# Attention and ResMLP over eight batches: W1's chunks taken forwards and backwards in turn, and the third batch's k, q and v loaded and flipped one pass earlier

## The chip, the cores and the metric

The kernel runs on one core of a Trainium2 chip. The time is the device time of one execution in microseconds (us), and the median of several executions is compared. The profile is that of one execution: its span runs from the first to the last instruction. The engines are PE (TensorE's matmuls; PEld is its weight loads), DVE (VectorE), ACT (ScalarE), POOL (GpSimd) and SP (SyncE); the last two mostly issue DMAs here.

## The reference

For each of eight batches, grouped-query attention is computed and its output goes through a ResMLP block. The shapes are 16 query heads, 4 key heads, 384 positions and 64 elements per head, so that the attention output is 384 x 1024; W1 is 1024 x 4096 and W2 is 4096 x 1024. Everything comes in and goes out as float32.

```python
attn = softmax(q @ k.T / sqrt(D)) @ v            # each key head serves four query heads
x = attn.transpose(0, 2, 1, 3).reshape(B, S, H * D)
a1 = alpha1 * x + beta1
u = x + lam * einsum('ts,bsd->btd', w_tok, a1)
a2 = alpha2 * u + beta2
out = u + lam * (maximum(a2 @ w_ch1, 0.0) @ w_ch2)
```

## The kernel before

After a lead in which the first batch's attention and token mixing are done (`side(0)`), there are eight passes, one for each batch. Pass b is `main(b)`: the **first product** h = relu(a2 @ W1), L417 to L452, and the **second product** ch = h @ W2 with the output, L453 to L469. While it runs, the attention and token mixing of batch b + 1 (`side(b + 1)`) are set between its matmuls.

The first product takes 32 column blocks `nt` of 128 columns. Each is eight matmuls (L424) of a W1 block with a2T (384 columns; 385 in the first pass), then a bias and a relu on ACT or DVE into hT, which holds all 32 blocks. Two blocks are a **chunk** of W1 (512 KB in bfloat16), so there are 16 chunks. W1 is not kept: a ring of six tiles (`RING`) is refilled on POOL's queue by DMAs that read float32 and write bfloat16 (`load_w1`, L149). When chunk c is used up, its slot takes the chunk six further on. At the end of a pass that is the first six chunks of the next one (L438 and L439; L445 to L447 in the first pass). W2 is loaded once: three of its 16 parts in the lead, thirteen after chunk 10 of the first pass (L440 to L444), all of them at L154. The second product (L461) has six groups of 32 matmuls with 512 columns, in the order of `nt`; its output is scaled and added by DVE (L466, L467) and written by SP (L468).

The order of instructions is written by hand and holds for each engine's queue. `main` is a generator that yields after each few matmuls; the yields of the first product count the units of one list, those of the second product the units of another. `side(b + 1)` gives the two lists, from unit to work. For most batches the list for the first product is empty. For batch 1 it has the key and query transposes on TensorE with `k_transpose` (L208) and `q_transpose` (L218) in units 8 to 40, for batch 2 the query transposes in units 24, 32, 40 and 48 (L368). A `q_transpose` is six matmuls and a copy by DVE.

From batch 3 on (and for batch 2's k) there are no transposes on TensorE. q, k and v are loaded on POOL's queue (`load_q` L131, `load_k` L106, `load_v` L125; `load_next` does all three) and k and q are turned by transposing DMAs on SP's queue (`flip_k` L134, `flip_q` L138). These are added to the lists in L605 to L610: load in unit 2 of the second product of pass b for batch b + 2, `flip_k` in unit 34, `flip_q` in units 36, 37, 42 and 43. Batch 2 is apart: k is loaded at the end of the first pass (L448), q after chunks 1 to 4 and v after chunk 10 of the second pass (L449 to L452), and k is flipped in unit 1 of the second pass. a2 goes to a2T by transposing DMAs on SP too (L312), in the second product, one for each of eight slices.

The tiles `q_raw` and `k2` have one buffer each, v has two (`vt`). All the waits between engines, for loads and for buffers, are set by the framework from which instruction reads or writes what.

Of the kernel before, what the change touches and what calls it, by code (L numbers as in the profile page):

```python
# [12 lines left out]
def kernel(  # L13
# [21 lines left out]
    nc = tc.nc  # L35
    f32 = mybir.dt.float32
# [12 lines left out]
    P = 128  # L49
# [22 lines left out]
    ident = const.tile([P, P], bf, tag="ident", name="ident")  # L72
    vt = [const.tile([P, NST, Hkv, D1], bf, tag=f"v{i}", name=f"v{i}") for i in range(2)]
    w2 = const.tile([P, NNT, DM], bf, tag="w2", name="w2")
    hT = const.tile([P, NNT, S], bf, tag="hT", name="hT")
    hTf = hT.rearrange("p n s -> p (n s)")
    vecs = const.tile([P, 4, DM], f32, tag="vecs", name="vecs")
# [45 lines left out]
    def load_v(b, sts=range(NST)):  # L123
        for st in sts:
            nc.gpsimd.dma_start(out=vt[b % 2][:, st, :, :D], in_=by_st(v[b])[:, st])  # L125

    def load_q(b, hs=range(0, Hq, G)):
        if b not in qrs:
            qrs[b] = sb.tile([P, Hq, NST, D], bf, tag="q_raw", name="q_raw", bufs=1)
        for h in hs:  # L130
            nc.gpsimd.dma_start(out=qrs[b][:, h:h + G], in_=q[b, h:h + G].rearrange("h (p st) d -> p h st d", st=NST))  # L131

    def flip_k(b):
# [6 lines left out]

    w1src = moe_w_ch1.rearrange("(dt di) nf -> di dt nf", di=P)
    w2src = moe_w_ch2.rearrange("(nt ni) d -> ni nt d", ni=P)
    w1_tiles = {}

    def load_w1(n):
        if n < B * NCH:
            t = sb.tile([P, NDT, CW * P], bf, tag="w1", name="w1", bufs=RING)
            c = n % NCH
            nc.gpsimd.dma_start(out=t, in_=w1src[:, :, c * CW * P:(c + 1) * CW * P])  # L149
            w1_tiles[n] = t  # L150

    def load_w2(dw, i, n):
        r, cs = slice(i * NNT // n, (i + 1) * NNT // n), slice(dw * 512, (dw + 1) * 512)
        nc.gpsimd.dma_start(out=w2[:, r, cs], in_=w2src[:, r, cs])  # L154

    def bank(shape, tag, name, dtype=f32):
        if tag == "three":
            return threes[0].tile(shape, dtype, tag="sc", name=name, bufs=3)
        if tag == "mm":
            return mms.tile(shape, dtype, tag="mm", name=name, bufs=2)  # L160
        return psum.tile(shape, dtype, tag=tag, name=name, bufs=2 if tag == "sc" else 1)

    def three():
        return bank([P, 2, 4, P], "three", "sc")

    def tp_ps(shape, tag="tp"):
        return bank(shape, tag, "tp", bf)
# [9 lines left out]
    def h_part(nts, dts):  # L177
        for nt in nts:
            if nt % 2 == 0 and nt not in early:
                t = bank([P, 2, 512], "sc", "h")  # L180
                early[nt], early[nt + 1] = t[:, 0], t[:, 1]
            for dt in dts:
                nc.tensor.matmul(out=early[nt][:, :S + 1], lhsT=w1_tiles[nt // CW][:, dt, nt % CW * P:(nt % CW + 1) * P],  # L183
                                 rhs=a2Ts[0][:, dt, :S + 1], start=(dt == 0), stop=(dt == NDT - 1))


# [2 lines left out]
    def side(b):  # L189
# [175 lines left out]
        if not first:  # L365


            turns = {24 + 8 * i: [(q_transpose, 2 * i, 2, "three")] for i in range(4)} if b == 2 else {}  # L368
            if b == 1:
                turns = {4: [(to_all, 3, 0, 0), (to_all, 3, 1, 1), (load_row_set, 1, 1, 0), (load_row_set, 2, 0, 1)],  # L370
                         8: [(k_transpose, 0)], 12: [(to_all, 1, 0, 2), (to_all, 1, 1, 0), (load_row_set, 2, 1, 0)],
                         16: [(scale_beta,)], 20: [(to_all, 2, 0, 1), (to_all, 2, 1, 0)],
                         24: [(q_transpose, 0, 2, "av")], 28: [(k_transpose, 2)]}
                for i in range(3):
                    turns[32 + 4 * i] = [(q_transpose, 2 + 2 * i, 2, "av")]
            return turns, {
                0: [(scores3, 0)], 4: [(av, 0)], 6: [(scores3, 1)], 8: [(tok_flip, 0)], 11: [(av, 1)],
                13: [(scores3, 2, True)], 15: [(av, 2)], 16: [(tok_flip, 1)], 18: [(tok_flip, 2)], 19: [(av, 3)],
                21: [(scores3, 3)], 23: [(tok_flip, 3)], 25: [(av, 4)], 27: [(scores3, 4)], 29: [(tok_flip, 4)],
                31: [(av, 5)], 33: [(scores3, 5, True)], 35: [(av, 6), (tok_flip, 5)], 37: [(av, 7)],  # L380
                39: [(tok_flip, 6)], 41: [(tok_flip, 7)]}
# [31 lines left out]
    def main(b):  # L413
        a2T = a2Ts[b % 2]
        x = xs.pop(b)
        n = S + 1 if b == 0 else S
        for c in range(NCH):  # L417
            w1 = w1_tiles.pop(b * NCH + c)
            for j in range(CW):
                nt = c * CW + j  # L420
                begun = b == 0 and nt in early
                ps = early[nt] if begun else bank([P, 512], "mm", "h")
                for dt in range(0 if begun else NDT):
                    nc.tensor.matmul(out=ps[:, :n], lhsT=w1[:, dt, j * P:(j + 1) * P],  # L424
                                     rhs=a2T[:, dt, :n], start=(dt == 0), stop=(dt == NDT - 1))
                    if dt == 3:
                        yield 0
                c1 = bias1[:, nt:nt + 1]
                if b == 0:
                    evac("DVE" if nt % 2 else "ACT")(out=c1, in_=ps[:, S:n])  # L430
                if nt % 2 == 0:
                    nc.scalar.activation(out=hT[:, nt, :], in_=ps[:, :S], func=RELU, bias=c1)  # L432
                else:
                    nc.vector.tensor_scalar(out=hT[:, nt, :], in0=ps[:, :S], scalar1=c1,  # L434
                                            scalar2=0.0, op0=ADD, op1=mybir.AluOpType.max)
                yield 0

            if b or c + RING < NCH:  # L438
                load_w1(b * NCH + c + RING)  # L439
            if b == 0 and c == NCH - RING:  # L440
                for i in range(3, 8):
                    load_w2(0, i, 8)
                for i in range(8):
                    load_w2(1, i, 8)  # L444
            if b == 0 and c == NCH - 1:  # L445
                for i in range(RING):
                    load_w1(NCH + i)  # L447
                load_k(2)  # L448
            if b == 1 and c in range(1, 5):  # L449
                load_q(2, [G * (c - 1)])  # L450
            if b == 1 and c == NCH - RING:
                load_v(2)  # L452
        for dw in range(NDW):  # L453
            cs = slice(dw * 512, (dw + 1) * 512)
            for ms in range(NST):
                ps = bank([P, 512], "mm", "ch")
                o = sb.tile([P, 512], f32, tag="tmp", name="o", bufs=4)
                last = (b, dw, ms) == (B - 1, NDW - 1, NST - 1)
                for lo, hi in ((0, 256), (256, 384), (384, 512)) if last else ((0, 512),):
                    for nt in range(NNT):  # L460
                        nc.tensor.matmul(out=ps[:, lo:hi], lhsT=hT[:, nt, ms * P:(ms + 1) * P],  # L461
                                         rhs=w2[:, nt, dw * 512 + lo:dw * 512 + hi], start=(nt == 0), stop=(nt == NNT - 1))
                        if nt % 4 == 3 and nt < NNT - 1:
                            yield 1
                    c = slice(dw * 512 + lo, dw * 512 + hi)
                    nc.vector.tensor_tensor(out=o[:, lo:hi], in0=ps[:, lo:hi], in1=lam_t[:, c], op=MUL)  # L466
                    nc.vector.tensor_tensor(out=o[:, lo:hi], in0=o[:, lo:hi], in1=x[:, ms, c], op=ADD)  # L467
                    nc.sync.dma_start(out=out[b].rearrange("(p st) d -> p st d", st=NST)[:, ms, c], in_=o[:, lo:hi])  # L468
                yield 1  # L469
# [3 lines left out]
    with tc.manual_schedule(engines=order):  # L473
# [128 lines left out]
        place_k(1, 1)  # L602
        for b in range(B):
            us = side(b + 1) if b + 1 < B else ({}, {})
            moves = [(0, 1, flip_k, 2)] if b == 1 else []  # L605
            if 0 < b < B - 2:
                moves += [(1, 2, load_next, b + 2), (1, 34, flip_k, b + 2), (1, 36, flip_q, b + 2, 0, 2),
                          (1, 37, flip_q, b + 2, 2, 2), (1, 42, flip_q, b + 2, 4, 2), (1, 43, flip_q, b + 2, 6, 2)]
            for i, u, *m in moves:
                us[i].setdefault(u, []).append(m)  # L610
            done = [0, 0]
            for second in main(b):
                if b == second - done[1] - 1 == 0:
                    lead_banks.close()
                    threes.append(ST(tc.psum_pool(name="threes", bufs=3)))
                for f, *a in us[second].get(done[second], []):
                    f(*a)
                done[second] += 1
# [28 lines left out]
```

## Time and profile before

| what | value |
|---|---|
| median of four runs | 802.69 us (801.8 to 802.83) |
| the profiled execution | 802.28 us |
| its span | 800.5 us |
| granted TensorE clock | 1.0 |
| HBM read / written | 172.92 MB / 12.58 MB |
| loads of W1 (L149) and W2 (L154) | 128 and 16, 512 KB each |
| starts of the first products, from the chain | 37.8, 131.5, 229.5, 326.2, 422.8, 519.5, 616.1, 712.8 us |

The profile has several views. The page gives each engine's busy time and share, and the span in 40 slices (tenths of a slice that the engine was busy, tenths of the clock that was granted, DMA load). The chain of waits follows the work that ended last back from the last instruction; in order of time it gives pieces by start, length, engine and line. Views by stretch give busy time between two moments, views by engine list instructions, and the view of waits says who waited for whom. For a DMA the trace has its issue and the time from issue to landing.

### The profile page before, as it was taken

How to read it: one execution, taken by the hardware profiler on the slowest of the kernel's cores; microseconds unless marked ns; L12 is line 12 of the kernel's file. 1: busy time of each engine (PE TensorE's matmuls, PEld its weight loads, DVE VectorE, ACT ScalarE, POOL GpSimd, SP SyncE). 2: the span in 40 equal slices, each digit the busy share in tenths (PEclk: the TensorE clock that was granted, in tenths of full speed). 3: DMA queues.
4: the chain of work that ended last, by engine and by line, in shares of the span. 5: the costliest groups of instructions: out<-in, count | busy, mean ns of one | idle time of the engine just before them, and what ended most of it. 6: DMA issues, size and time to landing. Idle time of an engine off the chain costs nothing.

```text
span 800.5 us, 14229 instructions
## 1 busy us (share of the span) xinstructions
PE 793.7 (99%) x6131; PEld 452.7 (57%) x6131; DVE 347.3 (43%) x676; ACT 223.1 (28%) x302; POOL 181.4 (23%) x232
## 2 busy tenths in 40 slices
PE   8999999999999999999999999999999999999997
PEld 5765555655556555565555655566555655556545
DVE  7663555226542266323662235622465225552122
ACT  7623340232412332123221234122421223312100
POOL 9434311451013400235002340033300330003000
PEclk9999999999999999999999999999999999999999
DMA  9999999999279963999439992599914994139411
GB/s 191 197 199 203 213 205 147 184 195 178 58 133 185 197 98 69 151 189 196 84 82 143 197 199 49 101 156 198 175 47 114 177 197 80 47 67 182 57 40 40
DMA packets 234875, 112.42 MB, mean 140 GB/s; under 512 B 87348, under 2 KB 228644, under 8 KB 234812
## 3 DMA queue, kind: packets, MB, share of 16 engines
q0 software_dynamic: 177088, 85.83, 81.6%
q1 hardware_dynamic: 57180, 25.29, 12.8%
q8 instruction: 48, 0.79, 0.4%
q10 hardware_dynamic: 544, 0.39, 0.2%
q14 instruction: 15, 0.12, 0.0%
HBM read 172.92 MB, written 12.58 MB: 232 GB/s over the span
## 4 chain that ended last, share of the span: by engine, by line
PE 98%; DVE 2%; issue 0%; ACT 0%
PE ch L461 42%; PE h L424 41%; PE sc L232 4%; PE sc L267 4%; PE sc L290 4%; PE h L183 1%; PE tp L218 1%; PE tok L290 0%; PE av L267 0%; PE warm L478 0%; PE ut L307 0%; DVE x L273 0%; DVE vecs L348 0%; PE tok L294 0%; DVE hT L545 0%
## 5 line engine op out<-in xcount | busy, mean ns | idle before, releaser
L461 PE MATMUL ch<-w,hT 128*128 128x512 bf16 (+2 forms) x1600 | 357.7, 371 | 0.9 <-DVE o L466 0.9
L424 PE MATMUL h<-a2T,w 128*128 128x384 bf16 (+1 forms) x2016 | 330.8, 326 | 0.0
L424 PEld LDWEIGHTS <-w 128*128 128x128 bf16 x2016 | 196.5, 98 | 130.4 <-DMA w<-in_moe_w_ch_dram 0.3
L461 PEld LDWEIGHTS <-hT 128*128 128x128 bf16 x1600 | 144.6, 98 | 152.7 <-issue 10.0
L149 POOL DMA_DIRECT2D w<-in_moe_w_ch_dram x128 | 112.2, 878 | 507.4 <-PE h L424 492.2
L241 ACT ACTIVATE es<-sc 128x1024 bf16<-128x1024 f32 x126 | 121.4, 1023 | 187.7 <-PE sc L232 178.8
L434 DVE TENSOR_SCALAR hT<-h,bias 128x384 bf16<-128x384 f32 x128 | 79.1, 618 | 214.6 <-PE h L424 214.1
L432 ACT ACTIVATE hT<-h,bias 128x384 bf16<-128x384 f32 x128 | 74.3, 580 | 304.2 <-PE h L424 303.6
L466 DVE TENSOR_TENSOR o<-ch,vecs 128x512 f32<-128x512 f32 (+2 forms) x50 | 33.4, 669 | 109.1 <-PE ch L461 109.1
L267 PEld LDWEIGHTS <-es 128*128 128x128 bf16 x1008 | 38.2, 97 | 13.2
L290 PEld LDWEIGHTS <-wtokT 128*128 128x128 bf16 x576 | 37.4, 98 | 12.3 <-DVE a L280 1.7
L232 PE MATMUL sc<-qT,kT 64*128 64x384 bf16 (+2 forms) x576 | 42.3, 272 | 0.7 <-DVE qT L220 0.4
L272 DVE RECIPROCAL rinv<-sc 128x6 f32<-128x6 f32 x56 | 10.8, 193 | 67.3 <-PE sc L267 66.3
L267 PE MATMUL sc<-v,es 128*128 128x65 bf16 x1008 | 39.8, 193 | 0.0
L297 DVE TENSOR_TENSOR x<-sc,x 128x384 f32<-128x384 f32 x56 | 31.0, 553 | 20.0 <-PE sc L290 20.0
L290 PE MATMUL sc<-a,wtokT 128*128 128x128 bf16 x504 | 37.3, 219 | 0.0
L232 PEld LDWEIGHTS <-kT 64*128 64x128 bf16 x576 | 21.7, 94 | 24.6 <-issue 19.6
L467 DVE TENSOR_TENSOR o<-o,x 128x512 f32<-128x512 f32 (+2 forms) x50 | 33.5, 671 | 1.7
L301 DVE TENSOR_TENSOR a<-x,vecs 128x384 bf16<-128x384 f32 x56 | 31.3, 558 | 1.9
L278 DVE TENSOR_TENSOR a1f<-x,vecs 128x384 f32<-128x384 f32 x56 | 31.2, 558 | 1.9
L280 DVE TENSOR_TENSOR a<-a1f,vecs 128x384 bf16<-128x384 f32 x56 | 31.2, 558 | 1.9
L273 DVE TENSOR_TENSOR x<-sc,rinv 128x384 f32<-128x384 f32 x56 | 31.2, 558 | 1.9
(84 smaller groups left out, 209.0 us busy)
## 6 DMA issues: line engine op xcount, KB each, us to landing
w<-in_moe_w_ch_dram POOLq DMA_DIRECT2D x144, 512.0 KB, 8.9
out_dram<-o SPq DMA_DIRECT2D x47, 256.0 KB, 2.4
q_raw<-in_q_dram POOLq DMA_DIRECT2D x28, 192.0 KB, 11.4
k<-in_k_dram POOLq DMA_DIRECT2D x12, 192.0 KB, 10.4
v<-in_v_dram POOLq DMA_DIRECT2D x24, 64.0 KB, 8.7
a2T<-a SPq DMA_TRANSPOSE x56, 2.6
hT<-in_k_dram SPq DMA_DIRECT2D x4, 192.0 KB, 5.2
qg<-in_q_dram POOLq DMA_DIRECT2D x3, 192.0 KB, 4.7
```

Source lines behind the costliest of these rows:

```text
L149: nc.gpsimd.dma_start(out=t, in_=w1src[:, :, c * CW * P:(c + 1) * CW * P])
L232: nc.tensor.matmul(out=sc[:, hh, k % 4:k % 4 + n], lhsT=kT[r, 2 * p // G, BLK[hh][sk], :], rhs=qT[r, p, st:st + n, :], start=True, stop=True)
L241: nc.scalar.activation(out=e, in_=sc, func=EXP, scale=scale_qk)
L267: nc.tensor.matmul(out=av[:, hh, sq, :], lhsT=ess[k // 4][:, m % 2, k % 4, :], rhs=vb[:, sk, hk, :], start=(sk == 0), stop=(sk == NST - 1))
L290: nc.tensor.matmul(out=ps[:, tt, :], lhsT=wtokT[:, st, tt * P:(tt + 1) * P], rhs=a1s[p][:, st, :], start=(st == 0), stop=(st == NST - 1 an ...
L301: nc.vector.tensor_tensor(out=a2s[p], in0=u, in1=bc(al2, p), op=MUL)
L424: nc.tensor.matmul(out=ps[:, :n], lhsT=w1[:, dt, j * P:(j + 1) * P], rhs=a2T[:, dt, :n], start=(dt == 0), stop=(dt == NDT - 1))
L432: nc.scalar.activation(out=hT[:, nt, :], in_=ps[:, :S], func=RELU, bias=c1)
L434: nc.vector.tensor_scalar(out=hT[:, nt, :], in0=ps[:, :S], scalar1=c1, scalar2=0.0, op0=ADD, op1=mybir.AluOpType.max)
L461: nc.tensor.matmul(out=ps[:, lo:hi], lhsT=hT[:, nt, ms * P:(ms + 1) * P], rhs=w2[:, nt, dw * 512 + lo:dw * 512 + hi], start=(nt == 0), sto ...
L466: nc.vector.tensor_tensor(out=o[:, lo:hi], in0=ps[:, lo:hi], in1=lam_t[:, c], op=MUL)
L467: nc.vector.tensor_tensor(out=o[:, lo:hi], in0=o[:, lo:hi], in1=x[:, ms, c], op=ADD)
```

## The change

The ring of six tiles becomes one tile `w1` with six slots and a list of free ones. The odd passes take the chunks from 15 down to 0, the even ones from 0 up to 15, and a slot is refilled only while its own pass still has chunks to load. So the last six chunks of a pass stay where they are, and they are the first six of the next pass. The second product goes through `nt` in the order of the first one.

The third batch (b = 2) becomes like the later ones: k, q and v are loaded by `load_next(2)` in the first pass, right behind the thirteen loads of W2, and k and q are flipped on SP in the second product of the first pass, in the same units as in later passes. Its query transposes on TensorE go, and so do its loads among the chunks of the second pass. `bank` and `three` are only written shorter.

```diff
+    w1 = const.tile([P, RING, NDT, CW * P], bf, tag="w1", name="w1")
...
-    def load_w1(n):
-        if n < B * NCH:
-            t = sb.tile([P, NDT, CW * P], bf, tag="w1", name="w1", bufs=RING)
-            c = n % NCH
-            nc.gpsimd.dma_start(out=t, in_=w1src[:, :, c * CW * P:(c + 1) * CW * P])
-            w1_tiles[n] = t
+    w1_slots, w1_free = {}, list(range(RING))
+
+    def load_w1(c):
+        w1_slots[c] = w1_free.pop(0)
+        nc.gpsimd.dma_start(out=w1[:, w1_slots[c]], in_=w1src[:, :, c * CW * P:(c + 1) * CW * P])
...
-            turns = {24 + 8 * i: [(q_transpose, 2 * i, 2, "three")] for i in range(4)} if b == 2 else {}
+            turns = {}
...
-        for c in range(NCH):
-            w1 = w1_tiles.pop(b * NCH + c)
+
+        seq = list(range(NCH))[::-1 if b % 2 else 1]
+        for i, c in enumerate(seq):
...
-                    nc.tensor.matmul(out=ps[:, :n], lhsT=w1[:, dt, j * P:(j + 1) * P],
+                    nc.tensor.matmul(out=ps[:, :n], lhsT=w1[:, w1_slots[c], dt, j * P:(j + 1) * P],
...
-            if b or c + RING < NCH:
-                load_w1(b * NCH + c + RING)
-            if b == 0 and c == NCH - RING:
-                for i in range(3, 8):
-                    load_w2(0, i, 8)
-                for i in range(8):
-                    load_w2(1, i, 8)
-            if b == 0 and c == NCH - 1:
-                for i in range(RING):
-                    load_w1(NCH + i)
-                load_k(2)
-            if b == 1 and c in range(1, 5):
-                load_q(2, [G * (c - 1)])
-            if b == 1 and c == NCH - RING:
-                load_v(2)
+            if i + RING < NCH:
+                w1_free.append(w1_slots.pop(c))
+                load_w1(seq[i + RING])
+
+            if b == 0 and i == NCH - RING:
+                for r in range(3, 8):
+                    load_w2(0, r, 8)
+                for r in range(8):
+                    load_w2(1, r, 8)
+                load_next(2)
+        nts = [c * CW + j for c in seq for j in range(CW)]
...
-                    for nt in range(NNT):
+                    for i, nt in enumerate(nts):
...
-            moves = [(0, 1, flip_k, 2)] if b == 1 else []
-            if 0 < b < B - 2:
-                moves += [(1, 2, load_next, b + 2), (1, 34, flip_k, b + 2), (1, 36, flip_q, b + 2, 0, 2),
-                          (1, 37, flip_q, b + 2, 2, 2), (1, 42, flip_q, b + 2, 4, 2), (1, 43, flip_q, b + 2, 6, 2)]
-            for i, u, *m in moves:
-                us[i].setdefault(u, []).append(m)
+            moves = []
+            if b < B - 2:
+                moves = [(2, load_next, b + 2)] if b else []
+                moves += [(34, flip_k, b + 2), (36, flip_q, b + 2, 0, 2), (37, flip_q, b + 2, 2, 2),
+                          (42, flip_q, b + 2, 4, 2), (43, flip_q, b + 2, 6, 2)]
+            for u, *m in moves:
+                us[1].setdefault(u, []).append(m)
```

More of the change, by code (lines that the diff above doesn't have):

```diff
@@ L125, in load_v, with load_q @@
             nc.gpsimd.dma_start(out=vt[b % 2][:, st, :, :D], in_=by_st(v[b])[:, st])
[L127 to L130, printed above, removed]
+    def load_q(b):
+        qrs[b] = sb.tile([P, Hq, NST, D], bf, tag="q_raw", name="q_raw", bufs=1)
+        for h in range(0, Hq, G):
             nc.gpsimd.dma_start(out=qrs[b][:, h:h + G], in_=q[b, h:h + G].rearrange("h (p st) d -> p h st d", st=NST))
@@ L142 @@
     w2src = moe_w_ch2.rearrange("(nt ni) d -> ni nt d", ni=P)
-    w1_tiles = {}
-    def load_w1(n):
-        if n < B * NCH:
-            t = sb.tile([P, NDT, CW * P], bf, tag="w1", name="w1", bufs=RING)
-            c = n % NCH
-            nc.gpsimd.dma_start(out=t, in_=w1src[:, :, c * CW * P:(c + 1) * CW * P])
-            w1_tiles[n] = t
+    w1_slots, w1_free = {}, list(range(RING))
+    def load_w1(c):
+        w1_slots[c] = w1_free.pop(0)
+        nc.gpsimd.dma_start(out=w1[:, w1_slots[c]], in_=w1src[:, :, c * CW * P:(c + 1) * CW * P])
     def load_w2(dw, i, n):
@@ L156, in bank @@
     def bank(shape, tag, name, dtype=f32):
-        if tag == "three":
-            return threes[0].tile(shape, dtype, tag="sc", name=name, bufs=3)
         if tag == "mm":
@@ L163, in three @@
     def three():
-        return bank([P, 2, 4, P], "three", "sc")
+        return threes[0].tile([P, 2, 4, P], f32, tag="sc", name="sc", bufs=3)
     def tp_ps(shape, tag="tp"):
@@ L182, in h_part @@
             for dt in dts:
-                nc.tensor.matmul(out=early[nt][:, :S + 1], lhsT=w1_tiles[nt // CW][:, dt, nt % CW * P:(nt % CW + 1) * P],
+                nc.tensor.matmul(out=early[nt][:, :S + 1], lhsT=w1[:, w1_slots[nt // CW], dt, nt % CW * P:(nt % CW + 1) * P],
                                  rhs=a2Ts[0][:, dt, :S + 1], start=(dt == 0), stop=(dt == NDT - 1))
@@ L459, in main @@
                 for lo, hi in ((0, 256), (256, 384), (384, 512)) if last else ((0, 512),):
-                    for nt in range(NNT):
+                    for i, nt in enumerate(nts):
                         nc.tensor.matmul(out=ps[:, lo:hi], lhsT=hT[:, nt, ms * P:(ms + 1) * P],
-                                         rhs=w2[:, nt, dw * 512 + lo:dw * 512 + hi], start=(nt == 0), stop=(nt == NNT - 1))
-                        if nt % 4 == 3 and nt < NNT - 1:
+                                         rhs=w2[:, nt, dw * 512 + lo:dw * 512 + hi], start=(i == 0), stop=(i == NNT - 1))
+                        if i % 4 == 3 and i < NNT - 1:
                             yield 1
```

## The prediction

> **What bounds the kernel now.** I read the busy shares and the slices first, then the chain of waits, then that chain in order of time.
>
> ```profile
> PE 793.7 (99%) x6131; PEld 452.7 (57%) x6131; DVE 347.3 (43%) x676; ACT 223.1 (28%) x302; POOL 181.4 (23%) x232
> ...
> PEclk9999999999999999999999999999999999999999
> DMA  9999999999279963999439992599914994139411
> ```
>
> TensorE is busy for 793.7 of 800.5 us at the full granted clock. The DMA engines are at nine tenths or more in many slices, so two resources look full. The chain says which of them sets the end:
>
> ```profile
> PE 98%; DVE 2%; issue 0%; ACT 0%
> ```
>
> No DMA is in it. The end moves only by what leaves, or is added to, TensorE's own row of work. In order of time this is the first product of the second pass (b = 1), in pieces of start, length, engine, line and count:
>
> ```profile
> 147.73 0.33 PE tp L218 x6
> 148.06 5.20 PE h L424 x32
> 153.27 0.33 PE tp L218 x6
> 153.60 5.20 PE h L424 x32
> 158.80 0.33 PE tp L218 x6
> 159.13 5.28 PE h L424 x32
> 164.41 0.33 PE tp L218 x6
> 164.75 9.75 PE h L424 x60
> ```
>
> Four groups of six transposes (L218, the third batch's q) stand between the matmuls of L424, and one block of 32 matmuls takes 5.28 instead of 5.20 us. Stretch by stretch (from:to, length, then busy time of PE, PEld, DVE, ACT, POOL, the granted clock, the DMA share, GB/s):
>
> ```profile
> 131.48:174.50 43.02, 43.02 (x281) 26.28 (x280) 12.88 (x21) 9.29 (x16) 18.42 (x22) 1.00 1.34 177
> 229.54:271.14 41.60, 41.60 (x257) 25.02 (x256) 10.66 (x17) 9.30 (x16) 13.12 (x15) 1.00 1.31 180
> ...
> 76.43:131.48 55.05, 55.05 (x482) 29.45 (x480) 30.65 (x60) 17.34 (x18) 8.97 (x11) 1.00 1.25 198
> 174.50:229.54 55.04, 55.04 (x482) 29.44 (x481) 30.48 (x59) 17.34 (x18) 7.56 (x10) 1.00 0.80 125
> ```
>
> The first two rows are the first product of the second and the third pass: 43.02 against 41.60 us. The chain gives 41.60 for all later passes too. The last two are the second product of the first and the second pass: 55.05 and 55.04, though only the second of them holds the flips of k and q (L134, L138) on SP.
>
> **What the change removes from TensorE.** From the 43.02 us go 24 transposes. Their gaps in the chain are 0.33 to 0.34 us a group, so 4 x 0.335 = 1.34 us, or 56 ns a transpose (the 219 ns that the groups give as the mean of one is a pipelined duration). The other 0.08 us belongs to this row, the only wait of a first product for a chunk of W1:
>
> ```profile
> PEld L424 <- DMA w<-in_moe_w_ch_dram: 0.3, 1, 0.3
> ```
>
> It lies at 163.58 us. A chunk's load is issued when its slot comes free and must land before TensorE has done the five other chunks in the ring, 5 x 16 x 162.5 ns = 13.0 us later. In this stretch the loads landed 12.7 to 13.4 us after issue, because q and v of the third batch were queued among them; in the next pass they took 5.6 to 8.2 us. The q and v loads leave this stretch, so this wait goes: 1.34 + 0.08 = 1.42 us, just the difference 43.02 - 41.60.
>
> The Trainium skill prices a transpose otherwise: "TensorE: Matmul & The Clock Gate", Part 4 (PE-mode transpose), has about 275 ns for one in a kernel, which as an estimate would make 24 x 275 ns = 6.6 us; the same page's section on the back-to-back issue gap has about 81 ns for a sustained matmul of 128 columns, an estimate of 1.9 us. The chain's 56 ns speaks against both, and the sum doesn't use them.
>
> **What it removes from the DMA queue.** Loads of W1 go from 128 to 16 + 7 x 10 = 86. With 42 fewer, POOL issues for some 42 x 0.87 = 37 us less and 22 MB less are written. I cost that at nothing, from both sides. A gain would need matmuls that run faster when DMA is quiet: the first product takes 41.60 us at a DMA share of 1.31 (third pass) and 41.60 at 0.99 (last pass), and a 512-column matmul takes 215.8 ns both in the block before the third pass (5.18 us for 24) and in the last pass, where the DMA share is 0.08. A loss would need a chunk that comes later: loads 7 to 16 of each pass are issued at the same points as now, behind less. In the first pass nothing that is issued up to W2's last load (83.16) changes, so W1's chunks land there some 10.5 us after issue as now.
>
> **Backwards order.** The number of matmuls, their shapes and their pauses are the same. The rows of hT that a pass overwrites first were read by matmuls that TensorE, which works in order, has already done; the second product takes nt in the order in which the first made them, so its last operand is as fresh as now. Zero either way; both ends of its cost come from the equal 55.04 us above and stay within 0.01 us.
>
> **What is moved into the first pass.** POOL issues nine loads (two k, four q, three v) behind the 13 of W2, where six of W1 and two of k stand now. One wait is new: the q tile has one buffer, and its last reader, the last group of transposes in this pass, runs at 63.7 us (in the chain the piece of 16 matmuls from 61.07 ends at 63.68, the next starts at 64.02). POOL gets to the first q load after W2 and k, past 88 us; behind it stand three q, three v and then only W1's loads of the second pass, from 134 us. It costs nothing. The last load of W2 lands 22.6 us after issue, at 105.8. In the second pass the same nine had landed 9.9 us after the last W1 chunk (188.7 to 198.6); so here about 115.7, with k near 108.7 and the first q near 110.2. When are they needed? This is SP in the second pass (start, length, line, what it issues):
>
> ```profile
> 214.77 1.44 SPq L134 DMA_TRANSPOSE kT<-k  x1
> 220.27 1.19 SPq L312 DMA_TRANSPOSE a2T<-a  x1
> 221.57 2.96 SPq L138 DMA_TRANSPOSE qT<-q_raw  x2
> 224.63 0.52 SPq L468 DMA_DIRECT2D out_dram<-o  x1
> 225.26 2.50 SPq L312 DMA_TRANSPOSE a2T<-a  x2
> ```
>
> The second product starts at 174.50 there and at 76.43 in the first pass, 98.07 earlier: the flip of k would go at 116.7, q's first at 123.5. k has 8 us to spare and q 13. The flips hold the last two a2T transposes back by some 0.8 us (50.76 against 50.00 us after the product's start); the second and later passes live with that and show no stall in L424. Cost: 0, from the equal 55.05 and 55.04; the upper end is the slower rival below.
>
> **The sum.** The profiled execution took 802.28 us, of which 800.5 are span and 1.78 lie around it. The span becomes 800.5 - 1.42 = 799.1 and the time 800.86. The four runs shown have a median of 802.69 (801.8 to 802.83), 0.41 above the profiled one; from it the sum is 801.27. I take 801.2, between the two and nearer to the median. That is 0.18% below it. I count a difference under 0.2%, 1.6 us, as one that a measurement of this kernel can't tell from none, so the forecast lies just inside that.
>
> **Rivals.**
> 1. *The flips arrive in a crowded queue* (slower). While DMA is loaded, an a2T transpose issued at 122 us in the first pass landed in 6.9 us instead of some 2.3. If the nine loads are still running when the last two a2T are issued (ending 53.26 us into the product, at 129.7), these land at 136.6; the first product of the second pass starts at 131.48 and needs its last a2T slice 7 x 0.1625 = 1.14 us later, at 132.6. TensorE stalls for 4.0 us: 801.2 + 4.0 = 805.2. For it: in the present kernel the queue is full until 128.7. Against it: what fills it from 105.8 is the six W1 chunks that leave. It decides only if the loads land past some 123 us, 7 us later than reckoned. 0.04.
> 2. *W1 as one tile is waited for as a whole* (slower by far). A chunk's matmuls would wait for the latest load into any slot: about 5.6 - 2.6 = 3 us for each of ten chunks in seven passes, 200 us and more, some 1010 us. Against it: w2 is one tile too, and L461 starts at 76.43 while its loads are issued up to 83.16 and land up to 105.8. 0.02.
> 3. *The gap is refilled* (no change). The transposes also gave W1's chunks time. If these still come 13 us after issue, TensorE waits for DMA for what it no longer transposes: 802.3 to 802.7. For it: the 0.3 us wait above. Against it: the loads that made them late leave. That the flips don't replace the transposes would read the same. 0.05.
> 4. *A transpose costs more than its gap*. Taking the weight load's 98 ns as its price gives 24 x 98 ns = 2.35 us, 800.3. Against it: the chain's gaps hold both. 0.05.
>
> **How the numbers follow.** The forecast has 0.84. Its own spread is that of the runs: 801.8 - 1.42 = 800.4 to about 802. It misses the 1.6 us by 0.2, while the four runs lie 1.03 apart and two medians of such runs can well differ by 0.4; so I give a third and a bit of it, 0.30, to faster and 0.54 to the same. With rival 4, faster is 0.35; with rival 3, the same is 0.59; rivals 1 and 2 make slower 0.06. The range takes in rival 4 at its low end and most of rival 3: 800.2 to 802.4, and leaves out the two slower ones.
>
> **What would show it.** Right: L218's groups for q_raw fall from 48 transposes to 24; the first product of the second pass takes 41.60 us; the wait of L424 for a DMA is gone; the pieces from 0 to 131.5 us and the second products stay as they are; w issues fall from 144 to 102. Wrong: a stall ahead of L424 just after 131.5 us (rival 1), waits of L424 for w within passes (2 or 3), or a first product of the second pass that is still 43 us.

## The result and the profile after

The changed kernel took 800.35 us (median of 36 runs, 799.93 to 802.34) against 802.29 us for the kernel before (54 runs, 801.04 to 804.66). The medians differ by 1.94 us; the ratio is 0.998, with a 95% interval of 0.9975 to 0.9985. The profiled execution took 800.70 us with a span of 798.9. The time lies in the predicted range (800.2 to 802.4), 0.85 us under the forecast.

In the new program the first product is L420 (L424 before), the second L452 (L461), the query transposes are L213 (L218) and the a2T flips L307 (L312). The engine, the DMA and the chain rows of the page after:

```profile
PE 791.8 (99%) x6107; PEld 451.6 (57%) x6107; DVE 345.8 (43%) x672; ACT 223.0 (28%) x302; POOL 144.4 (18%) x190
...
DMA  9999996991289713995149921499014961139311
...
PE 95%; DMA 2%; POOL 1%; DVE 1%; ACT 0%; issue 0%; DVEq 0%
```

TensorE is the bound as before; it has 24 instructions fewer and is busy for 1.9 us less. POOL issues 37 us less; the issues of W1 and W2 fall from 144 to 102. DMA moves 91.18 MB where it moved 112.42, and HBM reads are 128.88 MB instead of 172.92, but the end moved by 0.2% only. The DMA and POOL steps that are now in the chain lie before 41.5 us, in the lead and the first 5 us of the first product. The chain around the second pass:

```profile
125.89 5.18 PE ch L452 x24
131.07 41.60 PE h L420 x256
172.67 0.86 PE ch L452 x4
```

And the two stretches that were 55.05 and 43.02 us before (columns as in the prediction; the windows are set some hundredths of a microsecond beside the chain's pieces, which give 55.04 and 41.60):

```profile
76.03:131.10 55.07, 55.07 (x482) 29.48 (x481) 30.65 (x60) 17.34 (x18) 9.63 (x13) 1.00 1.13 180
131.09:172.67 41.58, 41.58 (x257) 25.03 (x256) 10.67 (x17) 9.30 (x16) 15.44 (x19) 1.00 1.32 171
```

The first product of the second pass has no transposes, no wait, and the 41.60 us of every later pass. The second product of the first pass now holds the flips and is as long as it was. SP's queue there:

```profile
116.31 1.44 SPq L134 DMA_TRANSPOSE kT<-k  x1
121.75 1.18 SPq L307 DMA_TRANSPOSE a2T<-a  x1
123.02 2.57 SPq L138 DMA_TRANSPOSE qT<-q_raw  x2
125.69 0.53 SPq L459 DMA_DIRECT2D out_dram<-o  x1
126.31 2.50 SPq L307 DMA_TRANSPOSE a2T<-a  x2
```

The flips go out at their planned places and take 1.2 to 1.4 us each. DMA is little loaded by then: the last v load is issued at 108.37 us and lands 8.3 us later, at about 116.7, and the DMA share is 0.49 from 116 to 122 us and 0.62 from 122 to 128. The experiments below show the same flips beside more traffic.

From the start of the first pass's second product to the last piece but one of TensorE there are 792.91 - 76.43 = 716.48 us in the profile before and 791.09 - 76.03 = 715.06 after: 1.42 us. The other 0.40 us lie before 76 us, in the lead and the first product of the first pass, where TensorE has the same work in both programs. Below, "the lead" stands for all that lies before this second product.

### The profile page after: what moved, and what is told of

It reads as the page before. It is cut to its first block, busy times and chain, and to the rows that moved or that the text cites. A ratio compares the mean times of both kernels' runs of the same rounds, so it can differ in the third digit from the quotient of the medians.

```text
span 798.9 us, 14094 instructions
## 1 busy us (share of the span) xinstructions
PE 791.8 (99%) x6107; PEld 451.6 (57%) x6107; DVE 345.8 (43%) x672; ACT 223.0 (28%) x302; POOL 144.4 (18%) x190
## 2 busy tenths in 40 slices
DMA packets 194394, 91.18 MB, mean 114 GB/s; under 512 B 89876, under 2 KB 188164, under 8 KB 194332
## 3 DMA queue, kind: packets, MB, share of 16 engines
HBM read 128.88 MB, written 12.58 MB: 177 GB/s over the span
## 4 chain that ended last, share of the span: by engine, by line
PE 95%; DMA 2%; POOL 1%; DVE 1%; ACT 0%; issue 0%; DVEq 0%
PE ch L452 42%; PE h L420 41%; PE sc L227 4%; PE sc L262 4%; PE sc L285 4%; DMA w<-in_moe_w_ch_dram 2%; DMA rows<-in_moe_lam_dram 1%; PE warm L469 0%; ACT hT L236 0%; POOL w L147 0%; POOL w L151 0%; PE tp L213 0%; DVE vecs L556 0%; DVE o L457 0%; POOL hT L541 0%
## 5 line engine op out<-in xcount | busy, mean ns | idle before, releaser
L452 PE MATMUL ch<-w,hT 128*128 128x512 bf16 (+2 forms) x1600 | 357.6, 371 | 0.9 <-DVE o L457 0.9
L420 PE MATMUL h<-a2T,w 128*128 128x384 bf16 (+1 forms) x2016 | 330.3, 326 | 0.3 <-DVE hT L430 0.3
L420 PEld LDWEIGHTS <-w 128*128 128x128 bf16 x2016 | 196.9, 98 | 131.0 <-DVE hT L430 0.7
L452 PEld LDWEIGHTS <-hT 128*128 128x128 bf16 x1600 | 144.7, 98 | 152.6 <-issue 10.1
L147 POOL DMA_DIRECT2D w<-in_moe_w_ch_dram x86 | 75.4, 879 | 533.7 <-PE h L420 532.3
L285 PEld LDWEIGHTS <-wtokT 128*128 128x128 bf16 x576 | 37.4, 98 | 12.3 <-DVE a L275 1.7
```

Of the source, the lines that this page charges most:

```text
L147: nc.gpsimd.dma_start(out=w1[:, w1_slots[c]], in_=w1src[:, :, c * CW * P:(c + 1) * CW * P])
L285: nc.tensor.matmul(out=ps[:, tt, :], lhsT=wtokT[:, st, tt * P:(tt + 1) * P], rhs=a1s[p][:, st, :], start=(st == 0), stop=(st == NST - 1 an ...
L420: nc.tensor.matmul(out=ps[:, :n], lhsT=w1[:, w1_slots[c], dt, j * P:(j + 1) * P], rhs=a2T[:, dt, :n], start=(dt == 0), stop=(dt == NDT - 1))
```

## The experiments

**The transposes' price.** The kernel before, with the four groups done twice:

```diff
-            turns = {24 + 8 * i: [(q_transpose, 2 * i, 2, "three")] for i in range(4)} if b == 2 else {}
+            turns = {24 + 8 * i: [(q_transpose, 2 * i, 2, "three")] * 2 for i in range(4)} if b == 2 else {}
```

> The kernel before with each of the four groups of six query transposes of the third batch done twice (same result written again). It measures the price of a transpose on TensorE by itself. By the chain's gaps, 24 more transposes cost 1.34 us: first product of the second pass 44.3 to 44.4 us. By the Trainium skill's 81 ns a piece it would be 1.9 us, and by 275 ns 6.6 us. A refilled gap (the loads set the pace in this stretch) would show as less than 1.3 us, or as the 0.3 us wait for W1 gone.

Measured: 802.77 us, ratio 1.0007 (0.9998 to 1.0016), which alone couldn't tell. The chain can:

```profile
147.04 0.67 PE tp L218 x12
147.71 5.20 PE h L424 x32
152.91 0.67 PE tp L218 x12
153.58 5.20 PE h L424 x32
```

Twelve transposes take 0.67 us, six took 0.33: 56 ns each, and all blocks of 32 are 5.20 us, the one of 5.28 too, since the later matmuls left W1's chunk time to land: the wait of L424 for W1 is gone. The stretch is 44.28 us (130.79 to 175.07), 1.26 longer, which is 1.34 - 0.08. By the terms of the expectation this is a refilled gap, of 0.08 us and no more. The Trainium skill's figures of 81 ns ("TensorE: Matmul & The Clock Gate", Back-to-back issue gap) and 275 ns (Part 4, PE-mode transpose) don't hold as the price of these transposes.

**The ring's turn alone**: the full change, with the third batch loaded and turned as before.

```diff
...
-                load_next(2)
+            if b == 0 and i == NCH - 1:
+                load_k(2)
+            if b == 1 and i in range(1, 5):
+                load_q(2, [G * (i - 1)])
+            if b == 1 and i == NCH - RING:
+                load_v(2)
...
```

> The full change with the third batch put back: one W1 tile, every other pass backwards, 86 loads of W1, but k, q and v of the third batch loaded and q transposed on TensorE in the second pass as before. Theory A: no change in time, within 0.3 us of before; first product of the second pass 42.9 to 43.1 us, all other stretches equal. Theory B: 0.4 to 0.5 us under before, and the later first products or the stretch up to 76 us shorter than before.

Measured: 802.25 us, ratio 1.0006 (0.9997 to 1.0015). The median lies 0.38 us above that of before, a little more than the 0.3 I allowed, with 1 inside the interval. TensorE's stretch says it more finely: the first product of the second pass takes 42.94 us (131.49 to 174.43), as expected, and from the start of the first pass's second product to the last piece but one there are 716.41 us against 716.48 before. The 0.07 us are the wait for W1, which is gone here too. So 42 loads fewer gain nothing beyond that: theory A.

**The move alone**: the old ring, the nine loads behind W2, the six W1 loads behind those.

```diff
...
             if b == 0 and c == NCH - RING:
...
+                load_next(2)
             if b == 0 and c == NCH - 1:
                 for i in range(RING):
                     load_w1(NCH + i)
-                load_k(2)
...
```

> The kernel before with the second half of the change alone: the third batch's k, q and v are loaded behind W2 in the first pass and flipped in its second product, no transposes in the second pass; the ring stays as it was and all 128 loads of W1 stay, with the six for the second pass behind the nine loads. Theory A: the whole gain without the ring's turn: first product of the second pass 41.60 us, no wait of L424's for W1, time 1.4 us under before and equal to the full change within 0.4 us. Theory B (the 42 loads that leave are worth something themselves, which is why the measured 1.94 us are more than 1.42): 0.5 us slower than the full change.

Measured: 814.08 us, ratio 1.0151 (1.0137 to 1.0165). Neither theory had that: the half that holds the whole gain is 12 us slower than before when it stands alone. TensorE at the start of its second pass:

```profile
130.94 1.14 PE L424 MATMUL h<-a2T,w 128*128 128x384 bf16 x6
140.14 0.48 PE L424 MATMUL h<-a2T,w 128*128 128x384 bf16 x1 [8.06 <-DMA a2T<-a]
142.56 7.63 PE L424 MATMUL h<-a2T,w 128*128 128x384 bf16 x29 [1.93 <-DMA a2T<-a]
```

It does six matmuls and then waits 8.06 and 1.93 us for the last two slices of a2T, the wait that the first rival named. SP shows how they became late:

```profile
116.34 3.18 SPq L134 DMA_TRANSPOSE kT<-k  x1
121.79 1.21 SPq L312 DMA_TRANSPOSE a2T<-a  x1
123.08 5.99 SPq L138 DMA_TRANSPOSE qT<-q_raw  x2
129.17 0.53 SPq L464 DMA_DIRECT2D out_dram<-o  x1
129.80 3.17 SPq L312 DMA_TRANSPOSE a2T<-a  x2
```

k and q were there in time (k's flip goes at 116.34, as in the full change). But the six W1 loads now run beside them: the DMA share is 1.37 from 116 to 122 us, where the full change has 0.49. k's flip takes 3.18 us of SP instead of 1.44, two of q's 5.99 instead of 2.57, and they land 12.8 (k) and up to 11.6 us (q) after issue instead of 3.7 and 2.8. The last two a2T go out from 129.80 to 132.97 us and land at about 140.1 and 142.5. The stall then costs twice, by the granted clock (the column before the DMA share):

```profile
131.00:142.50 11.50, 1.56 (x8) 0.63 (x7) 1.38 (x2) 0.00 (x0) 0.00 (x0) 0.65 1.34 195
142.50:148.00 5.50, 5.45 (x18) 2.59 (x18) 0.62 (x1) 0.58 (x1) 0.88 (x1) 0.50 0.75 101
148.00:154.00 6.00, 6.00 (x38) 3.61 (x37) 1.23 (x2) 1.69 (x3) 1.75 (x2) 0.98 1.09 140
```

For 5.5 us after the wait TensorE is granted half its clock. The first product of the second pass takes 54.8 us (131.1 to 185.9), 11.8 more than before; 10.0 of it are the waits. The Trainium skill ("TensorE: Matmul & The Clock Gate", Why this matters for your kernels) says that a gap of more than some 3 us between matmuls takes the clock back to half. This row agrees; but two runs below lose clock after waits of 2.14 and 2.49 us, so here 3 us is no safe limit.

**The move with the nine loads behind the six**: the same, with `load_next(2)` after the W1 loads.

> As the run with the move alone, but the nine loads of the third batch stand behind the six loads of W1 instead of ahead of them. This is the first rival's case made on purpose. The six chunks landed up to 126 us in the kernel before, so k lands at some 129 and the first q at 131, while k's flip would go at 116.7 us. If SP is held by that flip and the last two a2T transposes stand behind it, they go out past 135 us and TensorE stalls at the start of the second pass (131.5 us) by 5 to 8 us: time 4 to 7 us over before. If it isn't held, the time is 1.4 us under before as with the loads ahead.

Measured: 811.20 us, ratio 1.0116 (1.0102 to 1.0130). k's flip waits on SP until 128.37 us, the last a2T go out at 136.66, and L424 waits 8.2 us in three pieces. The mechanism was as expected; with the clock's fall (0.50 from 136 to 143 us) it cost 9 us and not 4 to 7. Even so it is cheaper than the loads ahead: here the flips wait, but little runs beside the last a2T (DMA share 0.66 from 136 to 140.3 us), and the last lands 2.3 us after issue.

**Half of the six loaded again**: the full change, and

```diff
+            if b == 0 and i == NCH - 1:
+                for r in seq[-6:-3]:
+                    nc.gpsimd.dma_start(out=w1[:, w1_slots[r]], in_=w1src[:, :, r * CW * P:(r + 1) * CW * P])
```

> The full change, but three of the six chunks that stay in the ring are loaded again (same data into the same slots) behind the nine loads in the first pass: half the traffic that the ring's turn takes out of this stretch is put back, nothing else. Theory A2: the flips again run beside loads, and L424 waits for a2T at the start of the second pass, but less than with all six back: 2 to 7 us, time 802 to 807 us. Rival (it was the ring's old structure and not the traffic): no wait, time as with the full change, 800 to 801 us.

Measured: 801.47 us, ratio 0.9992 (0.9983 to 1.0001). The flips are slow again, and TensorE waits (a row of SP, then two of TensorE):

```profile
122.58 5.80 SPq L138 DMA_TRANSPOSE qT<-q_raw  x2
...
130.47 1.14 PE L420 MATMUL h<-a2T,w 128*128 128x384 bf16 x6
132.27 0.32 PE L420 MATMUL h<-a2T,w 128*128 128x384 bf16 x1 [0.66 <-DMA a2T<-a]
```

With 0, 3 and 6 chunks behind the nine loads, L424 or L420 waits 0, 0.8 and 10.0 us for a2T. For three the wait is smaller than the 2 to 7 us I expected, and the time lies under the 802 to 807 us: the last of the three chunks landed at about 129.3 us, just when the last two a2T went out (129.10 us and after). But the slow flips and the wait are there with the ring turned, so the traffic makes them without the old ring. All six chunks behind the nine loads in the turned ring were not tried; that the whole 10.0 us are traffic is likely and not shown.

**The move alone with the flips last**: in the first pass the flips stand in units 42 to 46, behind the a2T flips on SP.

```diff
...
+                at = (42, 43, 44, 45, 46) if b == 0 else (34, 36, 37, 42, 43)
+                moves += [(1, at[0], flip_k, b + 2)] + [(1, at[1 + i], flip_q, b + 2, 2 * i, 2) for i in range(4)]
...
```

> The run with the move alone (ring not turned, six W1 loads behind the nine; it took 814.08 us, with L424 waiting 10.0 us for a2T), but in the first pass the flips of k and q are issued in units 42 to 46, behind the last a2T transposes on SP's queue instead of ahead of them. Theory A2 (the stall is a2T queued behind flips that go slowly while the queue is full): the wait for a2T shrinks from 10.0 us to under 3 us and the time falls to 801 to 805 us. Rival (the full queue slows a2T by itself, whatever stands ahead on SP): the wait stays at 7 us or more. The flips in the crowded queue may still make later W1 chunks late.

Measured: 805.73 us, ratio 1.0043 (1.0029 to 1.0056). The wait for a2T falls from 10.0 to 2.8 us: most of it was the place on SP. The rest is the slow landing of a2T itself: in the chain the last one goes out at 127.7 us and lands at 135.55.

```profile
135.60 42.30 PE L424 MATMUL h<-a2T,w 128*128 128x384 bf16 x249 [2.49 <-DMA a2T<-a]
```

The time is 0.7 us above the 805 I allowed, and the clock accounts for it: 249 matmuls of 162.5 ns would take 40.46 us and take 42.30, at a granted clock of 0.53 from 135.6 to 138 us and 0.71 to 140. That is 2.8 + 1.8 - 1.4 = 3.2 of the 3.4 us by which TensorE's stretch is longer than before.

**The flips in place**: the kernel before, with q's flips in the second pass instead of its transposes.

```diff
...
-            moves = [(0, 1, flip_k, 2)] if b == 1 else []
+            moves = [(0, 1, flip_k, 2)] + [(0, 24 + 8 * i, flip_q, 2, 2 * i, 2) for i in range(4)] if b == 1 else []
```

> The kernel before with one edit: the third batch's queries are turned by SP's transposing DMAs in units 24, 32, 40 and 48 of the second pass, where TensorE's 24 transposes stood; all loads stay where they were. Theory A (the gain is the transposes' 1.34 us on TensorE plus the one wait of some 0.08 us): the first product of the second pass falls from 43.02 us towards 41.6, but q and v are still loaded among W1's chunks, which landed 12.7 to 13.4 us after issue against the 13.0 us that the ring allows, so some of it may come back as waits for W1; I expect 41.7 to 42.4. Theory C (the gap is refilled, the loads' place is what counts): TensorE waits for DMA for all that it no longer transposes, 42.9 to 43.1 us, and the time is that of before within 0.3 us.

Measured: 807.12 us, ratio 1.0067 (1.0055 to 1.0080); the stretch is 47.63 us, longer than with the transposes, which neither theory held. I had counted the gap that closes and not the flips' own traffic (three rows of TensorE and one stretch):

```profile
131.34 26.16 PE L424 MATMUL h<-a2T,w 128*128 128x384 bf16 x160
159.35 2.77 PE L424 MATMUL h<-a2T,w 128*128 128x384 bf16 x16 [1.85 <-DMA w<-in_moe_w_ch_dram]
164.26 14.85 PE L424 MATMUL h<-a2T,w 128*128 128x384 bf16 x80 [2.14 <-DMA w<-in_moe_w_ch_dram]
...
164.20:170.00 5.80, 5.74 (x25) 3.00 (x26) 0.62 (x1) 0.58 (x1) 2.23 (x3) 0.71 1.40 190
```

W1's chunks beside the flips land up to 18.3 us after issue where 13.0 are allowed. TensorE waits 1.85 and 2.14 us. After the second wait the granted clock is 0.71 on the mean from 164.2 to 170.0 us (0.53 to 0.57 up to 168, then 1.00). The waits make 4.0 of the 6.0 us above 41.60, the clock the rest.

**One batch further.** If flips cost nothing where DMA is little loaded, the second batch's 36 transposes in the first pass (2.0 us) are the next to go. The full change, and

```diff
-                         8: [(k_transpose, 0)], 12: [(to_all, 1, 0, 2), (to_all, 1, 1, 0), (load_row_set, 2, 1, 0)],
+                         12: [(to_all, 1, 0, 2), (to_all, 1, 1, 0), (load_row_set, 2, 1, 0)],
...
-                         24: [(q_transpose, 0, 2, "av")], 28: [(k_transpose, 2)]}
-                for i in range(3):
-                    turns[32 + 4 * i] = [(q_transpose, 2 + 2 * i, 2, "av")]
+                         8: [(flip_k, 1)]}
+                for i in range(4):
+                    turns[10 + 4 * i] = [(flip_q, 1, 2 * i, 2)]
```

> The full change, carried one batch further: the second batch's k and q, already in SBUF, are turned by SP's transposing DMAs in units 8 to 22 of the first pass, and the 36 transposes of that pass on TensorE go. If TensorE's row were all that counts, 36 x 56 ns = 2.0 us would go, and the time would be some 798.3 us. Theory A2 (a transposing DMA costs little in a quiet queue and much in a full one): the DMA share is 1.3 to 1.45 in this stretch and W1's chunks land some 10.5 us after issue against 13.0 allowed, so the flips push them over: L424 waits for W1 (or, in the second product, L461 for W2) by 3 to 9 us, and the time is 801 to 808 us, slower than the full change.

Measured: 807.40 us, ratio 1.0066 (1.0049 to 1.0083). The size was expected, the way was not: the wait was not for W1. A small load of alpha's row stood behind two flips on SP, DVE's shuffle waited 7.5 us for it (L556), and L420 6.6 us for DVE's evacuation. After it the granted clock was 0.50 to 0.55 from 59.1 to 65 us. The second try puts the flips in units 22 and 24 to 36, behind the row loads:

> As the run before it (second batch's k and q turned on SP in the first pass, no transposes on TensorE there), but the flips stand in units 22 to 36, behind the last load of the rows of alpha, beta and lam on SP's queue. In the run before, DVE's shuffle of those rows waited for a row load that stood behind two flips, and L424 lost 6.6 us to it. Theory A2: that wait is gone, and now the full queue shows: W1's chunks, which landed up to 18.3 us after issue beside the flips against 13.0 allowed, or W2's parts, are waited for by 2 to 6 us; time 800.5 to 805 us. If only the row loads had been in the way, 2.0 us under the full change, some 798.3 us, and a version faster than both kernels.

Measured: 806.77 us, ratio 1.0057 (1.0040 to 1.0074). That is 1.8 us above the top of what I expected. Now it is W1, in four waits of 1.0 to 2.0 us (5.9 us in all, then 1.3 us for W2 in L452), and the granted clock stays at 1.00 between and after them. Two of the four:

```profile
60.09 2.79 PE L420 MATMUL h<-a2T,w 128*128 128x385 bf16 x16 [1.02 <-DMA w<-in_moe_w_ch_dram]
64.36 2.79 PE L420 MATMUL h<-a2T,w 128*128 128x385 bf16 x16 [1.48 <-DMA w<-in_moe_w_ch_dram]
```

No version that I found beats the change.

**The change again**, for the lead:

> The full change once more, unaltered. Theory A: on TensorE it saves 1.42 us; what was measured above that (1.94 between the medians) is scatter of the lead, whose end (start of the first pass's second product) stood at 76.43 us before and 76.03 after in the two profiles. Then this run's second product can start anywhere from 75.3 to 76.5, the stretches from there on are equal to those of the first profile within 0.05 us, and the ratio comes out between 0.9975 and 0.9990. Theory B (a gain of its own in the lead or elsewhere): 76.0 again and 0.9975 or less.

Measured: 800.10 us, ratio 0.9983 (0.9972 to 0.9993). The second product starts at 75.33 us, 0.70 earlier than in the first profile of the same program, and from there to the last piece but one are 790.39 - 75.33 = 715.06 us, to the hundredth as in that profile. So the lead scatters by itself. The table has the end of the lead in every profile but the two of "One batch further", whose flips lie in it, and what TensorE needs from there to its last piece but one, where the scatter is left out:

| profile | start of the first pass's second product | from there to the last piece but one |
|---|---|---|
| before | 76.43 us | 716.48 us |
| transposes twice | 75.74 us | 717.75 us |
| ring alone | 76.44 us | 716.41 us |
| move alone | 76.02 us | 728.33 us |
| nine loads behind the six | 75.30 us | 726.19 us |
| half loaded again | 75.59 us | 716.20 us |
| move alone, flips last | 76.43 us | 719.89 us |
| flips in place | 76.45 us | 721.08 us |
| the change; the change again | 76.03; 75.33 us | 715.06; 715.06 us |

With the old ring the lead ends between 75.30 and 76.45 us, with the turned one between 75.33 and 76.44: no part of the change shows there. The chains differ early: the same step of DVE (vecs, L348 or L343) starts at 12.29 us in before and in the ring alone, and at 11.33 and 11.14 in the two of the change.

## Why the prediction held, point by point

- **The transposes and the wait, 1.34 + 0.08 us**: right, by the chain before and after (1.42 us) and by the doubled transposes. I laid the wait to the loads of q and v; it went with the ring alone too, which leaves them in this stretch. My "12.7 to 13.4 us" after issue holds for the loads issued from about 146 to 165 us; those before landed in 6.1 to 12.3, those behind in up to 13.8.
- **The 42 loads at nothing**: right as a price (ring alone: 1.0006, and 0.07 us in TensorE's stretch), incomplete as an account. I let them go as bytes that nobody waits for. Six of them would run just when the moved flips do, and with them there the move costs 12 us.
- **The moved loads and flips at nothing**: right for this kernel. The flips went 0.4 to 0.5 us before the planned 116.7 and 123.5, about as much as the lead was shorter, and the nine loads were through at some 116.7 us, not 115.7.
- **The first rival**: the mechanism exists, at its place. Its condition was wrong. I wrote that it decides only if the nine loads land past 123 us; in the move alone k's flip went on time and it decided, by the six W1 loads that ran beside the flips. Its 4.0 us left out that the flips themselves slow down (10.0 us of wait) and that the clock falls after the wait. I did say that the six leaving chunks speak against it, and the runs bear that out.
- **The second and the fourth rival** (W1 waited for as one tile; 98 ns a transpose) are out: the passes with one tile take 41.60 us, and the doubled transposes cost 56 ns each.
- **The third rival** (the gap refilled) doesn't occur here: no first product waits for W1. That this is because the loads leave the stretch too is argued only, since no run drops the transposes, keeps the loads and adds no flips.
- **The size**: the medians differ by 1.94 us, 0.5 more than the sum. The means of all runs differ by 1.61 us (interval plus or minus 0.27), which holds 1.42. The lead, alike in both programs, ends anywhere in a window of 1.15 us in the profiles. That the rest is this scatter is likely and not shown: what sets the lead's end in an execution was not tried. By my own line of 1.6 us, below which I said no difference could be told, the outcome that I held less likely came (0.35 for faster, 0.59 for the same); with 36 and 54 runs the interval is narrower than I reckoned from four.

## What to carry to other kernels

When one resource sets the end, count what leaves it, but look at when the other one is free: two halves of a change can be worth 0 and -12 us alone and +1.4 together. A transfer that nobody waits for still has a price if something that is waited for runs beside it, or stands behind it on the issuing engine. Before work is moved from an engine to transposing DMAs, read the DMA share of the stretch where they will run.

## What the runs showed of the hardware

- A transposing DMA of four heads of q took 1.24 us of SP and landed in 2.8 us where DMA was little loaded. Beside W1's loads it landed in 8 to 12 us; in the move alone two then took 5.99 us of SP, while in the flips in place, 4 to 5 us apart, each still took 1.2. It also slowed the loads next to it: W1's chunks from 13 to 18 us.
- The granted clock fell to 0.50 for 5.5 us after waits of 8.1 and 1.9 us, to between 0.50 and 0.55 for 6 us after one of 6.6, to 0.53 for 2.4 us after one of 2.49, and to 0.71 on the mean of 5.8 us after waits of 1.85 and 2.14. Four waits of 1.0 to 2.0 us, some 4 to 5 us apart, and one of 0.66 us left it at 1.00.
- TensorE's pace did not change with the DMA traffic seen: 256 matmuls of 384 columns took 41.60 us at DMA shares of 0.99, 1.31 and 1.32.
